# A planned two-filter FFT kernel on one core: F in one transfer, an inverse step on the full array, a last row in halves, and a new order

## The chip, the cores and the metric

The kernel runs on one core of a Trainium2 chip. The time is the device time of one execution in microseconds (us); lower is better. A core has five instruction streams that run side by side and meet only at semaphores: TensorE (PE, matrix products into PSUM), VectorE (DVE), ScalarE (ACT), GpSimd (POOL, unused here but for start-up) and SyncE (SP), which issues nearly all DMA transfers here. The transfers themselves are carried by 16 DMA engines.

## The reference

Input `x` is 2048 rows (S) by 1024 columns (D) in bf16; `gate_w` has 1024 values; `A_w_r`, `A_w_i`, `B_w_r`, `B_w_i` are real and imaginary parts of two filters of 2048 by 513. `B_x` is not used.

```
g = sigmoid((x * gate_w).sum(-1, keepdims=True))
X = rfft2(x)                      # over rows and columns
a = irfft2(X * (A_w_r + 1j*A_w_i)).bfloat16
b = irfft2(X * (B_w_r + 1j*B_w_i)).bfloat16
out = g * a + (1 - g) * b
```

One forward transform serves both filters; the two inverse transforms are mixed row by row with the gate `g`.

## The kernel before, in words

All transforms are matrix products with constant matrices (`make_consts`), in five stages. The 2048 rows are split as 128 partitions by 16 values of `n2`; the row transform is done in two factors, 128 and 16.

**S1** (`xrows`, `stage_s1`). `x` comes in eight transfers of two `n2` values (512 KB) each (`xload`). VectorE folds every pair of rows about the middle column (`fS`, `fT`: sum and difference, four rows of 256 a call). TensorE then multiplies by the constant `F` (the factor-128 transform), 8 matmuls of 256 columns per `n2`; every product needs `F` and `-F`, and `C["F"]` holds both, 1 MB, loaded in four pieces `FP` between the loads of `x`. For `n2` 14 and 15 (`FULL`) VectorE folds once more (`u0`, `u1`) and 8 matmuls of 128 columns do. The result is copied from PSUM to SBUF (`Z`), by ScalarE or VectorE. `gate_row` uses 32-column matmuls for the gate.

**D and S2** (`stage_d`, `stage_s2`), per group `kg` of 16: the column transform (8 matmuls of 256 and two of 1 column, copy `Q`), then the factor-16 row transform (4 matmuls of 512 columns, copy `X`).

**Products and I1** (`prod`, `stage_i1`), per filter `b` and pair of groups `m` (8 of each): VectorE multiplies `X` by the filter (two `mul` of 2048 elements per partition, two `sum` of 1024 that subtract or add the halves). For the pairs in `SPLIT` the two `sum` are left out and TensorE does them with twice the matmuls. `I1`, the first inverse step, is done twice per pair, for the two halves `h` of `n2`: the matmuls give 64 output rows each, for the two groups of the pair on the two halves of the array's columns (`64 * r`, "128*64" in the profile). The result is copied to a buffer `ub` (`V`, 1024 elements per partition) and "turned": a DMA from SBUF to SBUF takes the 128 partitions of `ub` to 16 partitions of the buffer that the next stage reads (one `turn` of 256 KB per `h`, 32 in all).

**S** (`inverse`), per `n2`: `Sj0`, `Sj1` and `Sk1` (16 matmuls of 128 columns) give the mixed rows, copy `T`; `Dinv` (8 matmuls of 256) is the inverse column transform, copy `o`; VectorE unfolds with four add or subtract calls (`h0`, `h1`, `y0`, `y1`) for two `n2` at a time (one at a time for 14 and 15), and SP writes the rows out. All rows with `n2` below 8 need every turn with `h` = 0, the others every turn with `h` = 1.

**The order.** `P.add` collects 518 nodes. `Plan.run` simulates the five engines; the string `TABLE` gives, for each node in order of creation, its engine (p, a, v, g, s) and its due place, by which a free engine picks among the nodes that are ready. Buffers come from pools with limits (`ub`: 10 at a time) in a ring of 32 cells. `Sched.emit` writes each engine's instructions in the resulting order with semaphore waits. Which engine copies what, and when, is thus fixed in the program; on the chip only waits decide. Nearly all instructions are recorded at the lines of helpers: L493 (matmuls), L496 (VectorE on two tensors), L518 and L519 (copies by ScalarE and VectorE), L524 (DMA issues), so the profile's groups are told apart by tile names and shapes.

Of the kernel before, what the change touches and what calls it, by code (L numbers as in the profile page):

```python
# [10 lines left out]
AP = bass.AP  # L11
# [6 lines left out]
v80 a100 s90 s145 s200 s255 s310 s365 s420 s475 s530 s585 s640 s695 a240 s750 s805 s860 s915 s978 s1105 s1168 s1295  # L18
s1358 s1421 s1484 s1548 s1611 s1674 s1737 s1801 s1864 s1927 s1990 s2054 v90 p160 a612 p1815 a1862 v505 v444 p666
v774 p578 a712 v611 v672 p840 a953 p753 a861 v888 v948 p1022 a1130 p1109 a1222 v1088 v1028 p1284 a1405 p1197 a1313  # L20
v1305 v1244 p1378 a1496 p1466 a1588 v1379 v1439 p1640 a1771 p1553 a1679 v1513 v1573 p1728 a1869 p1839 v1947 v1708
v1648 v1782 v1855 p1970 a2039 p2070 a2135 p1926 a1991 p2058 p2014 v2091 p2166 p2114 v2199 p2288 p2245 a2321 p2393
v2426 p2508 v2532 s2109 s2172 s2298 s2362 s2488 s2551 s2615 s2678 s2741 s2804 s2868 s2931 s2994 s3057 s3121 s3184
p2300 a2414 p2523 a2631 p2414 a2529 p2703 v2810 v3052 v3226 v2939 v3166 p3501 a3636 s3745 p3328 a3453 s3562 p2610
a2724 p2883 a2995 p2789 a2904 p3062 a3178 v3288 v3515 v3401 v3575 p3767 a3910 s4020 p3681 a3819 s3928 p2969 a3087
p3242 a3361 p3149 a3270 p3415 a3544 v4096 v4270 v3983 v4210 p4477 a4642 s4752 p4387 a4551 s4660 p3587 a3727 p3853
a4002 p3940 a4093 p4206 a4368 v4792 v5019 v4905 v5079 p5372 a5509 s5618 p5192 a5326 s5435 p4294 a4459 p4569 v4678
p4660 a4774 p4933 a5051 v5487 v5714 v5600 v5774 p5897 a6009 s6119 p5983 a6101 s6210 p4840 a4960 p5106 a5234 p5278
a5417 p5551 a5692 v6062 v6235 v5948 v6175 p6737 a6870 s6979 p6478 a6595 s6705 p5458 a5600 p5724 v5834 p6069 a6192
p6391 a6504 v6870 v6997 v7057 v7184 p7353 a7466 s7575 p7439 a7557 s7666 p6184 a6298 p6650 a6778 p6298 a6412 p6564  # L30
a6687 v7258 v7372 p7698 a7892 s8001 p7526 a7719 s7829 v6984 p7168 v7245 v7833 v7846 v8467 v8477 v8533 v8520 v8559
v8546 v6296 v6523 v6409 v6583 p6823 a6961 s7071 p6909 a7053 s7162 v3635 v3862 v3749 v3923 p4033 a4185 s4294 p4119
a4276 s6412 v4444 v4618 v4330 v4557 p4753 a4866 s4975 p5019 a5143 s6539 v5253 v5427 v5139 v5366 p5638 a5783 s5893
p5810 a5918 s6476 v8199 v8373 v8086 v8313 p8456 v8569 s8698 p8698 v8805 s8934 v7599 v7772 v7485 v7712 p7871 a7984
s8093 p7957 a8075 s8184 v6757 v6643 p6996 a7189 s7299 p7180 a7374 s7483 v7859 v7972 p8284 a8477 s8587 p8111 a8305
s8414 p8543 a8619 p8653 v8704 v8746 p8587 v8683 p8829 v9070 v9328 s6602 p8044 a8167 v8433 v8487 p8565 a8760 v8919
v8966 p8066 a8966 v9036 v9083 p8089 a8569 v8713 v8760 p8784 p9148 p9208 a9260 p9410 a9519 p9630 p9719 p9798 a9824
p9941 v10073 v10247 v10308 v10381 v10556 s10629 p8853 p9103 p9187 v9214 p9537 a9645 p8934 p9064 p9142 a9169 p9278
v9387 v9825 v9765 v9899 v10187 s10261 p10118 p10202 p10336 a10362 p10474 a10586 p9366 p9498 p9624 v9651 p9803 a9916
v10797 v10736 v10917 v11038 s11111 p9675 p9759 p9891 v9959 p10386 a10495 p9896 p10029 p10113 a10139 p10248 v10442  # L40
v10616 v10676 v10857 v10977 s11051 p10341 p10561 p10645 a10678 p10827 a10952 p10068 p10163 p10241 a10268 p10650
a10769 v11158 v11098 v11232 v11406 s11480 p10600 p10738 p10822 a10861 p11133 a11246 p10777 p10915 p10999 a11044
p11226 a11337 v11466 v11527 v11600 v11723 s11797 p11004 p11088 p11220 v11292 p11446 a11554 p10954 p11049 p11128
a11154 p11313 a11429 v11663 v11784 v11857 v11931 s12005 p11401 p11533 p11617 a11645 p11755 a11863 v11991 v12025
v12072 v12173 s12220 p11572 p11638 p11698 a11737 p11857 a11966 v12106 v12139 v12207 v12254 s12301"""
# [13 lines left out]
def make_consts():  # L59
# [14 lines left out]
    C["F"] = np.stack([F, -F], 2).reshape(128, 4096)  # L74
# [68 lines left out]
    KI = KI.reshape(2, 2, 128, 2, 2, 8, 8).transpose(2, 0, 1, 3, 4, 6, 5).reshape(128, 1024)  # L143
# [140 lines left out]
class Node:  # L284
    def __init__(self, name, key, engs, build, reads, writes, after, alloc, dma):
        self.name, self.key, self.engs, self.build = name, key, engs, build
        self.reads, self.writes, self.after, self.alloc, self.dma = reads, writes, after, alloc, dma
        self.pre, self.place = set(), 0


class Plan:


    def __init__(self, arena, limit):
# [4 lines left out]
        self.free0 = (0.8, 1.0, 0.8, 0.8, 0.9)  # L299

# [20 lines left out]
    def run(self, table):  # L321
# [21 lines left out]
        dma_free = 0.0  # L343
# [100 lines left out]
def bass_gated_mix__spectral_gfnet__spectral_gfnet__prompt_kernel(  # L444
# [60 lines left out]
    def pe(name, ns, build, reads, writes, alloc=(), **kw):  # L505
        return P.add(name, cost(ns), lambda e: build(), reads, writes, alloc=alloc, **kw)
# [434 lines left out]
```

## Time and profile before

| what | value |
|---|---|
| median of 3 runs | 132.09 us (132.0 to 132.16) |
| the profiled execution, its own time | 131.37 us |
| its span, from the first to the last instruction | 129.5 us |
| mean granted TensorE clock | 0.991 |
| PE, DVE, ACT busy | 117.5, 107.5, 100.2 us |
| DMA | 14064 packets, 28.62 MB, 221 GB/s on average |

A row such as "L496 DVE TENSOR_TENSOR RING<-R 128x2048" is one group of instructions: the line of the helper, the engine, the operation, the tensor written, the tensors read and the shape (partitions by elements). `R` stands for the large SBUF tensors R1 to R5 (`x`, the constant `F`, the filters, `X`, the turned data and the last stage's buffers), `RING` for the ring of small buffers, `PS` for PSUM. A busy time counts overlapping instructions once. The end of a matmul is modelled: a single one of 512 columns is recorded as 0.38 us, while its successor starts 0.216 us after it.

### The profile page before, as it was taken

The numbers are of one execution on the slowest core, as the hardware profiler recorded it, in microseconds if no ns is written. First come the engines' busy times: TensorE is split into PE (matmuls) and PEld (weight loads), VectorE is DVE, ScalarE is ACT, GpSimd is POOL, SyncE is SP. The second block draws the span as 40 slices with busy tenths as digits, with TensorE's granted clock in tenths as the row PEclk, the third lists the DMA queues.
The fourth block names the chain that finished last, engine by engine and source line by source line (L and its number), as shares of the span: only waits on it lengthen the run. The fifth ranks groups of instructions, "written<-read, shape, count | busy, mean of one in ns | idle before, by whom it ended". The sixth has DMA issues, their size and how long they took to land.

```text
span 129.5 us, 2793 instructions
## 1 busy us (share of the span) xinstructions
PE 117.5 (91%) x1149; PEld 76.6 (59%) x1149; DVE 107.5 (83%) x155; ACT 100.2 (77%) x109; POOL 0.2 (0%) x4
## 2 busy tenths in 40 slices
PE   6687999899999999999999999999969999999710
PEld 2365786566544455445483555555659999999600
DVE  1386796417999997998899999998965899999992
ACT  4348898597999997999799958667335659999950
POOL 0000000000000000000000000000000000000000
PEclk9999999999999999999999999999999999999996
DMA  4999999999999997406348998987630004435474
GB/s 116 289 379 419 407 418 372 378 378 387 382 380 372 218 193 180 132 0 161 90 128 217 289 209 190 221 200 168 172 81 5 0 0 167 162 149 197 173 297 162
DMA packets 14064, 28.62 MB, mean 221 GB/s; under 512 B 1506, under 2 KB 5858, under 8 KB 14051
## 3 DMA queue, kind: packets, MB, share of 16 engines
q1 hardware_dynamic: 14048, 28.44, 70.2%
q8 instruction: 9, 0.15, 0.5%
q14 instruction: 5, 0.03, 0.1%
q10 hardware_dynamic: 2, 0.00, 0.0%
HBM read 15.85 MB, written 4.19 MB: 155 GB/s over the span
## 4 chain that ended last, share of the span: by engine, by line
PE 60%; DVE 20%; DMA 9%; issue 3%; SPq 3%; ACT 2%; DVEq 0%
PE PS L493 60%; DVE R L496 14%; DMA R<-in_A_x_dram 7%; DVE R L519 4%; SPq L524 3%; DMA R<-RING 3%; ACT R L518 2%; DVE RING L496 1%; DVE RING L519 1%; ACT RING L518 1%; DVEq L248 0%; DVE V L519 0%
## 5 line engine op out<-in xcount | busy, mean ns | idle before, releaser
L518 ACT ACTIVATE R<-PS 128x1024 bf16<-128x1024 f32 x52 | 50.9, 1028 | 12.9 <-PE PS L493 12.7
L518 ACT ACTIVATE RING<-PS 128x1024 bf16<-128x1024 f32 (+1 forms) x48 | 46.7, 1008 | 8.8 <-PE PS L493 8.8
L496 DVE TENSOR_TENSOR RING<-R 128x2048 bf16<-128x2048 bf16 (+1 forms) x48 | 47.8, 1043 | 6.2 <-DMA R<-in_A_x_dram 6.1
L493 PE MATMUL PS<-RING,SK 128*64 128x512 bf16 (+1 forms) x368 | 51.2, 382 | 0.1
L493 PEld LDWEIGHTS PS<-RING,SK 128*64 128x64 bf16 (+1 forms) x368 | 21.5, 108 | 24.3 <-issue 6.7
L493 PE MATMUL PS<-DM,R 128*128 128x256 bf16 (+1 forms) x256 | 27.4, 245 | 0.5 <-DMA R<-RING 0.5
L493 PEld LDWEIGHTS PS<-DM,R 128*128 128x128 bf16 x256 | 18.9, 97 | 5.7 <-issue 2.1
L519 DVE CAST R<-PS 128x1024 bf16<-128x1024 f32 (+1 forms) x16 | 15.2, 961 | 8.1 <-PE PS L493 8.1
L496 DVE TENSOR_TENSOR R<-R 128x1024 bf16<-128x1024 bf16 (+1 forms) x36 | 20.6, 626 | 0.3
L496 DVE TENSOR_TENSOR RING<-RING 128x1024 bf16<-128x1024 bf16 x28 | 18.2, 684 | 0.1
L493 PE MATMUL PS<-DI,R 128*128 128x256 bf16 x128 | 16.1, 273 | 1.3 <-ACT R L518 1.3
L493 PE MATMUL PS<-R,RING 128*128 128x256 bf16 (+1 forms) x128 | 14.5, 266 | 2.6 <-DVE RING L496 2.6
L493 PEld LDWEIGHTS PS<-R,RING 128*128 128x128 bf16 x128 | 11.4, 98 | 6.0 <-DVE RING L496 4.5
L493 PEld LDWEIGHTS PS<-DI,R 128*128 128x128 bf16 x128 | 11.7, 98 | 3.0 <-ACT R L518 1.6
L493 PE MATMUL PS<-RING,R 128*128 128x128 bf16 x128 | 9.3, 219 | 0.0
L493 PEld LDWEIGHTS PS<-RING,R 128*128 128x128 bf16 x128 | 7.7, 98 | 0.6 <-DVE R L519 0.4
L493 PE MATMUL PS<-MS,R 128*128 128x1 bf16 (+1 forms) x40 | 5.2, 165 | 0.0
L519 DVE CAST RING<-PS 128x512 bf16<-128x512 f32 (+1 forms) x4 | 3.8, 958 | 1.6 <-PE PS L493 1.5
L493 PE MATMUL PS<-RING 128*128 128x512 bf16 x8 | 3.5, 615 | 1.2 <-DVE RING L588 1.2
L493 PEld LDWEIGHTS PS<-MS,R 128*128 128x128 bf16 (+1 forms) x40 | 3.4, 96 | 0.4 <-issue 0.2
L844 ACT ACTIVATE RING<-PS 128x512 bf16<-128x512 f32 x4 | 2.4, 601 | 1.1 <-DVE RING L496 1.1
L493 PE MATMUL PS<-R,G 128*32 128x512 bf16 x32 | 2.5, 384 | 0.4 <-ACT R L518 0.4
(34 smaller groups left out, 17.7 us busy)
## 6 DMA issues: line engine op xcount, KB each, us to landing
R<-RING SPq DMA_DIRECT2D x32, 256.0 KB, 4.4
R<-in_A_x_dram SPq DMA_DIRECT2D x8, 512.0 KB, 8.3
out_dram<-R SPq DMA_DIRECT2D x7, 512.0 KB, 2.6
R<-in_A_w_r_dram SPq DMA_DIRECT2D x7, 256.5 KB, 9.6
R<-in_A_w_i_dram SPq DMA_DIRECT2D x7, 256.5 KB, 9.5
R<-in_B_w_i_dram SPq DMA_DIRECT2D x7, 256.5 KB, 8.1
R<-in_B_w_r_dram SPq DMA_DIRECT2D x7, 256.5 KB, 8.2
R<-c_F SPq DMA_DIRECT2D x2, 320.0 KB, 7.6
```

Of the source, the lines that this page charges most:

```text
L493: return lambda e: e.matmul(o, l, r, start=start, stop=stop, skip_group_check=True)
L496: return lambda e: e.tensor_tensor(out=o, in0=a, in1=b, op=op)
L518: return [lambda e: e.activation(o, i, ACT.Copy)]
L519: return [lambda e: e.tensor_copy(o, i)]
L524: lambda e: [lambda q, d=d, s=s: q.dma_start(d, s) for d, s in pairs()],
L844: P.add("sig", {"act": (0.5, 0.7)}, lambda e: [lambda e: e.activation(rg(gr, 0, [[1, 512]]), psl(t, 0, [[1, 512]]), ACT.Sigmoid)], [(t,)], ...
```

## The change: what it does

1. `F` alone is loaded, 512 KB in one transfer after the first two rows of `x`; VectorE makes `-F` in two calls (`FN`, 256 and 1792 elements per partition). `S1` waits for both.
2. For `n2` 0, 1, 14 and 15 (`SINGLE`) the folds are done one row at a time (four calls of 512 elements in place of two of 1024).
3. `I1` takes one group at a time on the whole width of the array (128 output rows). `KI`'s columns are reordered so that the two halves `h` lie on alternate partitions of the result, and each result is turned in two transfers of 128 KB, each from every second partition (64) to 8 partitions: 64 in all.
4. The last pair (1, 7) (`LATE`) goes in smaller parts: four `mul` of 1024 elements, `I1` in three calls per group, copies `V` of 512.
5. The last row, `n2` = 15, is finished in halves (`finish`): `Dinv`, the copy (`oh`, 512), `h0` and `h1` (256) are done twice, `y0` and `y1` (512) write two tiles, and two transfers of 128 KB take them out, one of them in pieces of 256 elements.
6. `Sj1` and `Sk1` are one call except in the first two rows of each half; one warm-up matmul fewer is issued; the pools change (`ub` 10 to 5, `q` 4 to 2, `st` 3 to 4 and others); `TABLE` has 554 new entries. In it VectorE has 13 copies of 1024 elements (3 `Z`, 2 `Q`, 1 `X`, 3 `T`, 4 `o`) and two `V` of 512, before 14 (2 `Z`, 3 `X`, 2 `V`, 4 `T`, 3 `o`).

```diff
-SPLIT = ((0, 7), (1, 6), (1, 7))
+SPLIT = ((0, 7), (1, 6))
+LATE = ((1, 7),)
+SINGLE = (0, 14)
-FP = ((0, 2), (2, 6), (6, 11), (11, 16))
+NEG = (0, 2, 16)
...
-    C["F"] = np.stack([F, -F], 2).reshape(128, 4096)
+    C["F"] = F.reshape(128, 2048)
...
-    KI = KI.reshape(2, 2, 128, 2, 2, 8, 8).transpose(2, 0, 1, 3, 4, 6, 5).reshape(128, 1024)
+    KI = KI.reshape(2, 2, 128, 2, 2, 8, 8).transpose(2, 0, 1, 3, 6, 5, 4).reshape(128, 1024)
...
-             {"ps": ("ps", 4), "p1": ("ps", 8), "sj": ("ps", 3), "st": ("ring", 3), "u": ("ring", 1), "q": ("ring", 4),
-              "t": ("ring", 2), "tn": ("ring", 4), "pp": ("ring", 2), "g": ("ring", 1), "gz": ("ring", 1), "RA": ("ring", 1), "ub": ("ring", 10), "w": ("ring", 1), "T": ("t", 4),
+             {"ps": ("ps", 4), "p1": ("ps", 8), "sj": ("ps", 3), "st": ("ring", 4), "u": ("ring", 2), "q": ("ring", 2),
+              "t": ("ring", 2), "tn": ("ring", 2), "tl": ("ring", 4), "pp": ("ring", 4), "g": ("ring", 2), "gz": ("ring", 2), "RA": ("ring", 1), "ub": ("ring", 5), "w": ("ring", 1), "T": ("t", 4),
...
     xload(*DEPTH[0])
-    for i, (a, b) in enumerate(FP):
-        cload("sp", R2, a * 256, "F", a * 256, b * 256, [("F", j) for j in range(a, b)])
-        if i + 1 < len(DEPTH):
-            xload(*DEPTH[i + 1])
-    for a, b in DEPTH[len(FP) + 1:]:
+    cload("sp", R2, 0, "F", 0, 2048, ["F"])
+    for a, b in DEPTH[1:]:
         xload(a, b)
...
+    for a, b in zip(NEG, NEG[1:]):
+        P.add("FN", {"dve": (0.07 + (b - a) * 0.034, 0.2 + (b - a) * 0.034)}, lambda e, a=a, b=b: [lambda e: e.tensor_scalar(
+            out=ap(R2, 2048 + a * 128, [[1, (b - a) * 128]]), in0=ap(R2, a * 128, [[1, (b - a) * 128]]), scalar1=-1.0, scalar2=None, op0=ALU.mult)],
+            ["F"], [("FN", i) for i in range(a, b)])
...
+        if (b, m) in LATE:
+            p = PT[b, m] = [[Tile("tl", 2) for _ in range(2)] for _ in range(2)]
+            for kg in range(2 * m, 2 * m + 2):
+                P.key = ("PA", "PB")[b], m
+                for c, t in enumerate(p[kg % 2]):
+                    P.add("mul", vt(1024), lambda e, t=t, c=c, kg=kg: [tt(
+                        rg(t, 0, [[512, 2], [1, 512]]), ap(R4, kg * 1024, [[512, 2], [1, 512]]),
+                        ap(T, kg * NS + c * NW, [[NW - 2 * c * NW, 2], [1, 512]]), ALU.mult)],
+                        [("X", kg)] + wkeys(b, (kg,)), [(t, 0, 2)], alloc=[t])
+            return
...
+        def turns(u, kg, parts=1):
+            for h in range(2):
+                def turn(h=h):
+                    return [(AP(T, (64 * (kg % 2) + m) * pt + h * 8192, [[8 * pt, 8], [1024, 8], [1, 1024]]),
+                             AP(RING, h * pit[id(RING)] + u.at * CELL, [[2 * pit[id(RING)], 64], [1, 1024]]))]
+                dma("turn", "sp", turn, 0.131, 200, [(u, i * 2 // parts, (i + 1) * 2 // parts) for i in range(parts)], [("U", b, kg, h)], n=1.1,
+                    after=allz(h) if b else [("x", i) for i in range(16)])
...
+        for r in range(2):
+            kg = 2 * m + r
+            P.key = ("IA", "IB")[b], kg
             t, u = Tile("ps", 2), Tile("ub", 2)
-            def fns(h=h, t=t):
...
-                            f.append(mm(psl(t, o * 512, [[1, 512]], 64 * r, 64), ap(SK, z, [[1, 64]]),
-                                        rg(src, r * 1024 + v, [[1, 512]]), i == 0, i == len(terms) - 1))
-                return f
...
+            def fns(r=r, t=t):
+                return [mm(psl(t, o * 512, [[1, 512]]), matrix(r, i, o * 128, 128), data(r, i), i == 0, i == len(terms) - 1)
+                        for o in range(2) for i in range(len(terms))]
...
             ev("V", 1024, lambda t=t, u=u: (rg(u, 0, [[1, 1024]]), psl(t, 0, [[1, 1024]])), [(t,)], [(u, 0, 2)])
-            dma("turn", "sp", lambda u=u, h=h: [(AP(T, m * pt + h * 8192, [[8 * pt, 16], [1024, 8], [1, 1024]]), rg(u, 0, [[1, 1024]]))],
-                0.262, 205, [(u, 0, 2)], [("U", b, m, h)], n=1.15, after=allz(h) if b else [("x", i) for i in range(16)])
+            turns(u, kg)
...
+    def finish(v, o, h):
+        for p in range(2):
+            P.key = ("E", 15)
+            t = Tile("p1", 1)
+            pe("Dinv", [256] * 4, lambda p=p, t=t: [
+                mm(psl(t, c * 256, [[1, 256]]), rg(v, (c * 4 + 2 * p + i) * 128, [[1, 128]]), ap(DI, ((2 * p + i) * 2 + c) * 256, [[1, 256]]), i == 0, i == 1)
+                for c in range(2) for i in range(2)], [(v, 0, 2), "DI"], [(t,)], alloc=[t] + ([] if p else [o]))
+            ev("oh", 512, lambda p=p, t=t: (rg(o, p * 512, [[1, 512]]), psl(t, 0, [[1, 512]])), [(t,)], [(o, p, p + 1)])
+            P.key = ("U", 15)
+            a, b = rg2(o, p * 512, [[1, 256]]), rg2(o, p * 512 + 256, [[1, 256]])
+            P.add("h0", vt(256), lambda e, p=p, a=a, b=b: [tt(rg(h, p * 512, [[1, 256]]), a(), b(), ALU.add)], [(o, p, p + 1)], [(h, p, p + 1)], alloc=[] if p else [h])
+            P.add("h1", vt(256), lambda e, p=p, a=a, b=b: [tt(rg(h, p * 512 + 511, [[-1, 256]]), a(), b(), ALU.subtract)], [(o, p, p + 1)], [(h, p, p + 1)])
...
+            d = outv[:, 15, 256:768] if i else AP(outv.tensor, outv[:, 15, 0:256].offset, [list(outv[:, 15, 0:256].ap[0]), [768, 2], [1, 256]])
+            dma("out", "sp", lambda y=y, d=d: [(d, rg(y, 0, [[1, 512]]))], 0.131, 400, [(y, 0, 1)], [], kind="out", n=0.65)
```

More of the change, by code (lines that the diff above doesn't have):

```diff
@@ L575, in wpart @@
         dma("W%d" % b, "sp", lambda: parts, 0.2627, 335, [], [("W", b, g, c, pm)], n=1.15 * len(parts),
-            after=[("F", i) for i in range(16)] if b and c == 0 and g < 2 else [])
+            after=["F"] + [("FN", i) for i in range(16)] if b and c == 0 and g < 2 else [])
     def wkeys(b, kgs=range(16)):
@@ L754, in stage_i1 @@
         pt = pit[id(T)]
[L755 to L776 removed]
+        wide = isinstance(p, list)
@@ L820, in v512 @@
             ev("U5", 8, lambda h=h: (ap(UR[b], 512 + h * 8192, [[1024, 8]]), psl(t2, h * 8, [[1, 8]])), [(t2,)], [("U5", b, h)], only="dve",
-               after=[("U", b, m, h) for m in range(8)])
+               after=[("U", b, kg, h) for kg in range(16)])
     for kg in range(16):
@@ L874, in inverse @@
             P.key = ("E", n2)
+            if last:
+                break
             def inv(t=t2, v=v):
```

149 lines of the change are left out of this document (91 added, 58 removed), and 2 rows, old and new, of the table P.

## The prediction

> **What bounds the kernel now.** I read the page first: its busy times, slices and chain.
>
> ```profile
> PE 117.5 (91%) x1149; PEld 76.6 (59%) x1149; DVE 107.5 (83%) x155; ACT 100.2 (77%) x109; POOL 0.2 (0%) x4
> PE   6687999899999999999999999999969999999710
> DVE  1386796417999997998899999998965899999992
> PE 60%; DVE 20%; DMA 9%; issue 3%; SPq 3%; ACT 2%; DVEq 0%
> ```
>
> See: PE is full from slice 5 to 28 (16 to 90 us), but DVE is nearly as full there, so PE alone does not set that stretch. The start waits for transfers; the end (slices 34 on) is DVE's. The timelines show the four places where this change acts. VectorE at the start:
>
> ```profile
> 4.33 1.29 DVE L496 TENSOR_TENSOR RING<-R 128x1024 bf16<-128x1024 bf16 x2 [3.18 <-DMA R<-in_A_x_dram]
> 6.82 1.29 DVE L496 TENSOR_TENSOR RING<-R 128x1024 bf16<-128x1024 bf16 x2 [1.19 <-DMA R<-in_A_x_dram]
> ...
> 11.48 1.29 DVE L496 TENSOR_TENSOR RING<-R 128x1024 bf16<-128x1024 bf16 x2 [0.90 <-DMA R<-in_A_x_dram]
> 13.59 5.14 DVE L496 TENSOR_TENSOR RING<-R 128x1024 bf16<-128x1024 bf16 x8 [0.81 <-DMA R<-in_A_x_dram]
> ```
>
> See: up to 13.59 each pair of rows waits for `x`, with pieces of `F` queued between. TensorE in the middle, one I1 between two groups D:
>
> ```profile
> 56.64 0.60 PE L493 MATMUL PS<-DM,R 128*128 128x256 bf16 x4
> 57.16 1.05 PE L493 MATMUL PS<-RING,SK 128*64 128x512 bf16 x8
> 58.15 0.50 PE L493 MATMUL PS<-DM,R 128*128 128x256 bf16 x3
> ```
>
> See: four matmuls of 256 columns follow one another at 0.109 us, so I1 could start at 57.07; it starts at 57.16. Its four pairs could take 4 x 0.216 = 0.86; D starts after 0.99. Going to half-width matmuls and back costs 0.09 + 0.12 = 0.21 to 0.22 us. And VectorE's only two waits between 31.13 and 88.14:
>
> ```profile
> 49.50 1.22 DVE L519 CAST R<-PS 128x1024 bf16<-128x1024 f32 x1 [0.89 <-PE PS L493]
> ...
> 62.10 1.22 DVE L519 CAST R<-PS 128x1024 bf16<-128x1024 f32 x1 [0.94 <-PE PS L493]
> ```
>
> Last, the chain of waits at the turn to the last stage:
>
> ```profile
> 89.97 1.22 DVE RING L519
> 91.19 0.03 DVE V L519
> 91.22 3.49 DMA R<-RING
> 94.71 0.05 issue
> 94.76 1.10 PE PS L493 x15
> ```
>
> See: the last products end at 88.14, the copy `V` at 91.19, its turn lands at 94.71, and only then the rows of S run on.
>
> **The change part by part.** The sum goes against the profiled execution, 131.37 us (span 129.5 plus 1.87 around it); the median of the runs is 0.72 above it.
>
> *Start.* In the trace the transfers land thus: x0 4.31, F 4.79, x1 6.80, F 7.96, x2 9.27, F 10.09, x3 11.38, F 12.21, x4 13.49, then one `x` every 1.28 to x7 at 17.34. New: x0 4.31, F (512 KB, as one `x`) 5.6, x1 6.9, then every 1.28: x4 10.7, x7 14.6. The first S1 comes later: F at 5.6 and `FN` for two rows, so 5.9 in place of 5.68. The second pair: 6.9 + 1.29 of folds = 8.2, as before (8.17). From there `x` (1.28) and folds (1.29) come faster than TensorE uses them (16 x 0.109 = 1.75 a pair), so six pairs end at 8.2 + 10.5 = 18.7, gfold 0.35 and the short pair 0.9 make 20.0. Before, S1 ends at 23.04 with two gate blocks and the products behind one in it (about 1.5): 21.5 for the same work. Gain 1.5. If the early rate (1.16 us for 256 KB of F) holds for the new F too, it lands at 6.6 and the gain is 0.8; without any wait 2.0. `FN` has no row: nearest are tensor-by-tensor calls, 1.09 us for 1792 elements by 0.69 per 1024 and 1.22 per 2048; from below 0.27, the one-source MEMSET. It lies between 5.9 and 6.9, where VectorE waits for x1: 0, at most 0.3. `SINGLE` adds two calls of about 0.1 twice, under the same waits. The missing warm-up matmul falls in an idle second (4.7 to 5.68): 0; if the clock were granted late, the first pair would run at the warm-ups' 0.427 per 512 columns, 1.75 more, 1.2 of it uncovered.
>
> *Middle.* There are 16 such visits to half width: TensorE is relieved of 16 x 0.22 = 3.5 us; the matmuls themselves are as long (a pair of halves 0.216, a full one 0.216). But VectorE works from 31.13 to 88.14 with 1.83 us of waits, and its work there does not shrink: three copies as before (2 `Q`, 1 `X` for 3 `X`), `LATE` 4 x 0.61 for 2 x 1.15 (+0.1). So at most 1.8 reaches the last product. Five visits (1.1 us) lie ahead of either wait, which would close both; another order may open others: I take half, 0.9 (0 to 1.8).
>
> *Turns and the passage to S.* SP issues 32 transfers more; one takes 0.53, 0.64 from start to start without a pause. In the last stretch, 16 turns from 73.41 to 93.60, 32 halves at 0.64 make 20.5 us in 20.2: SP just keeps up (0 to 0.6 late). A half turn is 0.64 us of transfer by bytes: ten whole turns land 1.19 apart from 79.62 to 90.29, and the sole one has 1.28. After the last `sum`, before 6.6 us pass until S runs on. New: I1 on one group 0.87, the other 0.87, its copy by ScalarE 1.03, three semaphore hops 0.1 to 0.2: 3.0; its first half turn then lands 2.4 after issue (3.0 for a whole one in the trace, less 0.64): 5.4. Gain 1.2; the other half queues behind three more issues (1.9), 7.3, where before the second half landed at 96.6, 8.5 after. Bounds 0 and 2.
>
> *S and the end.* From 100.69 to 127.0 VectorE never stops. It has seven copies as before; row 15 in halves gives 4 x 0.27 + 2 x 0.34 for 4 x 0.34: 0.3 more. The copies `oh` come 0.4 earlier and the last transfer is half as long (0.3 less). Together 0 (0.5 either way).
>
> Sum: 1.5 + 0.9 + 1.2 + 0 = 3.6; 131.37 - 3.6 = 127.8 for a profiled run, 128.5 for the median.
>
> **The rivals.**
>
> *A half turn costs as much as a whole one.* Then 32 of them at 1.2 take 38.4 us where 20.2 are there: 18 us later, 146.5. The gain is used up from 0.64 + 3.6/32 = 0.75 us on. Five buffers `ub` instead of ten would carry the delay back to TensorE. For it: the target has 8 partitions instead of 16, no row shows such a shape. Against it: the bytes halve, and the same 16 engines bring an `x` of 512 KB in 1.28, so a turn of 256 KB in 1.19 to 1.28 is not at their limit. Chance 0.17.
> [...]
> [...]
>
> *VectorE keeps the stretch.* The middle's waits only move and the passage gains nothing since SP's queue is late: only the start is left, 132.09 - 1.5 = 130.6. For it: 1.83 us of waits in 57. Against: both waits are for TensorE. Chance 0.22.
>
> *All of it pays.* 2.0 + 1.8 + 2.0 = 5.8: 126.3. Chance 0.06. *Nothing moves:* what the start gains is lost in a new order: 132.1, chance 0.03.
>
> **How the numbers follow.** My forecast has 0.52 and a range of its own of 127.0 to 130.3 (132.1 less 5.1 and less 1.8: start 2.0, middle 1.8, passage 1.3 against 0.8, 0.4, 0.6). The range for 8 in 10 leaves out the first rival and the edge of the third: 126.4 to 132.0. Two runs of this kernel differ by some 0.1%; 0.2% (0.26 us) is what can be told. Faster: 0.52 + 0.22 + 0.06, less 0.02 for the edge of the second, 0.78; same 0.03; slower 0.17 + 0.02 = 0.19.
>
> **What would show it.** F lands near 5.6 and x7 near 14.6; D's first matmul comes near 23 (before 24.81, with more gate work ahead of it). The middle has no half-width I1 and VectorE's span of products is 55 to 56 us. Turns land 0.6 to 0.7 apart when queued; S runs on 5 to 6 us after the last product. Wrong it would be if queued turns land over 0.75 apart, with TensorE waiting for copies `V` whose buffers are not free, or if VectorE waits for TensorE at new places in the middle. [...]

## The result and the profile after

The changed kernel takes 156.44 us (median of 4 runs, 155.74 to 156.96); the kernel before took 132.12 us beside it (132.0 to 132.3). The ratio is 1.1835, with a 95% interval of 1.1774 to 1.1897: 18% slower, where 128.5 us was forecast. Times of one kernel on one chip scatter by up to 0.7% either way (23 runs of the kernel before: 130.99 to 132.8 us), the changed kernel's relatives by more; where a ratio stands beside medians that don't match it, it leaves out disturbed runs, those more than 1.5% above the kernel's fastest.

The page of the changed kernel: the busy times, four of its slice rows (one slice is 3.86 us), the packets and the chain by engine.

```profile
PE 123.5 (80%) x990; PEld 79.5 (52%) x996; DVE 109.4 (71%) x164; ACT 99.9 (65%) x113; POOL 0.2 (0%) x4
...
PE   6599999999999765499767499519639999999930
...
PEclk9999999999999999879999969996995699999998
DMA  5999999999635555135855555555555000453337
GB/s 145 399 406 414 355 380 377 389 377 377 230 96 104 105 106 107 36 94 120 157 140 116 124 111 112 120 113 115 130 163 163 2 4 0 179 232 140 140 144 265
DMA packets 13902, 28.08 MB, mean 182 GB/s; under 512 B 1473, under 2 KB 6081, under 8 KB 13890
...
DMA 30%; PE 28%; DVE 20%; ACT 11%; issue 4%; SPq 4%; DVEq 0%; ACTq 0%
```

See: the engines' work is about the same as before (PE 123.5 for 117.5, part of it at a lower clock), but the span grew by 24.7 us and DMA now leads the chain (30%, before 9%). From slice 11 on (42 us) only half of the DMA engines' time is used, at 94 to 120 GB/s in most slices: these are the turns. Before, the stretch from 70 to 90 us ran at 214 GB/s. In the windows of the kernel before and then of the changed one (columns: stretch, its length, busy time of PE, PEld, DVE, ACT, POOL, granted clock, DMA share, GB/s):

```profile
70.00:90.00 20.00, 20.00 (x186) 10.20 (x184) 19.50 (x32) 15.40 (x17) 0.00 (x0) 1.00 0.95 214
```

```profile
70.00:90.00 20.00, 14.22 (x62) 5.81 (x62) 13.47 (x17) 11.69 (x15) 0.00 (x0) 0.95 0.60 132
90.00:115.00 25.00, 16.24 (x79) 6.92 (x79) 14.30 (x25) 10.87 (x15) 0.00 (x0) 0.91 0.53 122
115.00:125.00 10.00, 9.72 (x109) 8.97 (x110) 4.71 (x12) 3.13 (x4) 0.00 (x0) 0.66 0.24 74
```

See: TensorE and VectorE, almost without a pause before, stand for 30 to 40% of the time; and when the last stage starts (115 to 125 us), TensorE's granted clock is 0.66. What they wait for is in the list of waits of the changed kernel (us in total, times, the longest); the first and third lines have no counterpart before:

```profile
ACT RING L528 <- DMA R<-RING: 21.3, 12, 3.4
...
PE PS L501 <- ACT RING L528: 14.6, 9, 3.5
...
DVE RING L504 <- DMA R<-RING: 12.0, 4, 5.3
```

See: the copies `V` wait for a buffer `ub` whose turns have not landed, TensorE waits for those copies, and VectorE's products wait for cells of the same ring that turns have not freed. The chain names the same transfers; four of its pieces (start, length, what):

```profile
51.60 10.35 DMA R<-RING
...
82.06 10.58 DMA R<-RING
...
95.03 8.98 DMA R<-RING
...
105.77 7.45 DMA R<-RING
```

See: a half turn takes 7 to 10 us from its issue, because seven to nine others that were issued before it have not landed yet; with none ahead the first one took 3.3. The records of the trace give the price of one: in a queue the last packets of successive half turns come some 1.2 us apart (68.6, 69.7, 70.8, 71.9, 73.2), the landings 0.9 to 1.4, with eight engines at work and a median of 165 ns for a 2 KB packet. All 64 of them, 8.39 MB, take from 43.4 to 119.7 us; before, the same bytes took from 41.8 to 96.1.

| kernel | last product ends | last packet of a turn | span |
|---|---|---|---|
| before | 88.1 | 96.1 | 129.5 |
| changed | 105.7 | 119.7 | 154.2 |
| changed, partitions 4 apart, ten warm-ups (below) | 86.0 | 95.9 | 129.7 |

### The profile page after: what moved, and what is told of

The parts are those of the page before. It is cut to its first block, busy times and chain, and to the rows that moved or that the text cites. A ratio compares the mean times of both kernels' runs of the same rounds, so it can differ in the third digit from the quotient of the medians.

```text
span 154.2 us, 2529 instructions
## 1 busy us (share of the span) xinstructions
PE 123.5 (80%) x990; PEld 79.5 (52%) x996; DVE 109.4 (71%) x164; ACT 99.9 (65%) x113; POOL 0.2 (0%) x4
## 4 chain that ended last, share of the span: by engine, by line
DMA 30%; PE 28%; DVE 20%; ACT 11%; issue 4%; SPq 4%; DVEq 0%; ACTq 0%
PE PS L501 28%; DMA R<-RING 28%; DVE R L504 10%; DVE RING L504 7%; ACT RING L528 7%; ACT R L528 4%; SPq L534 4%; DMA R<-in_A_x_dram 2%; DVE R L529 2%; ACT RING L893 1%; DVEq L266 0%; DVE DM L504 0%; DVE R L602 0%; ACTq L252 0%; DVEq L252 0%
## 5 line engine op out<-in xcount | busy, mean ns | idle before, releaser
L501 PE MATMUL PS<-RING,SK 128*128 128x512 bf16 x210 | 54.8, 406 | 17.5 <-ACT RING L528 13.4
L504 DVE TENSOR_TENSOR RING<-R 128x2048 bf16<-128x2048 bf16 (+2 forms) x54 | 48.7, 946 | 25.2 <-DMA R<-RING 12.0
L528 ACT ACTIVATE R<-PS 128x1024 bf16<-128x1024 f32 (+1 forms) x54 | 52.3, 1017 | 17.5 <-PE PS L501 17.5
L501 PEld LDWEIGHTS PS<-RING,SK 128*128 128x128 bf16 x216 | 21.0, 103 | 45.7 <-ACT RING L528 12.9
L504 DVE TENSOR_TENSOR R<-R 128x1024 bf16<-128x1024 bf16 (+2 forms) x38 | 20.8, 603 | 0.3
L529 DVE CAST R<-PS 128x1024 bf16<-128x1024 f32 (+1 forms) x15 | 14.1, 947 | 6.0 <-PE PS L501 4.0
L501 PEld LDWEIGHTS PS<-R,RING 128*128 128x128 bf16 x128 | 12.3, 104 | 5.5 <-DVE R L602 2.7
L501 PE MATMUL PS<-RING,R 128*128 128x128 bf16 x128 | 10.8, 239 | 0.1
L529 DVE CAST RING<-PS 128x1024 bf16<-128x1024 f32 (+1 forms) x5 | 5.6, 1117 | 7.3 <-DMA R<-RING 4.3
L501 PEld LDWEIGHTS PS<-RING,R 128*128 128x128 bf16 x128 | 9.1, 108 | 0.5 <-DVE R L529 0.4
```

The costliest lines, as they stand in the source:

```text
L501: return lambda e: e.matmul(o, l, r, start=start, stop=stop, skip_group_check=True)
L504: return lambda e: e.tensor_tensor(out=o, in0=a, in1=b, op=op)
L528: return [lambda e: e.activation(o, i, ACT.Copy)]
L529: return [lambda e: e.tensor_copy(o, i)]
```

## The experiments

**Where the eight partitions lie.** A half turn has half the bytes of a whole one and costs as much. Was it the number of DMA engines (8 for 16), the places that it writes, or a fixed price? The two kernels here change only the numbering of the partitions of the turned data (with the rows of `RM`, the gate and the 512th column that go with it); sizes, outer counts, engines and order stay. The changed kernel writes eight partitions 8 apart, the two others eight 4 apart and eight side by side. The labels and the expectations call these layouts four, eight and two ports; a "port" there is a set of places taken to share a rate, the author's assumption, and no record shows one.

```diff
-AP(T, (64 * (kg % 2) + m) * pt + h * 8192, [[8 * pt, 8], [1024, 8], [1, 1024]])
+AP(T, (kg % 4 + 32 * (kg // 4)) * pt + h * 8192, [[4 * pt, 8], [1024, 8], [1, 1024]])   # 4 apart
+AP(T, (8 * kg) * pt + h * 8192, [[pt, 8], [1024, 8], [1, 1024]])                         # side by side
```

> The changed kernel, with another numbering of the partitions that the turns write: half turn kg goes to partitions kg mod 4 + 32 (kg div 4) + 4e, e = 0 to 7, in place of 64 (kg mod 2) + kg div 2 + 8e. Everything else stays, the shapes, the sizes and the outer counts of 64 and 8 too. Theory 1, the places of the target: the eight old partitions collide in pairs on the way into SBUF and the new ones do not; half turns land 0.62 to 0.70 us apart when queued (2 KB packets near 84 ns, as alone in the changed kernel), the waits for RING disappear, and the kernel takes 127 to 131 us, my forecast. [...] Theory 2, the number of DMA engines: it is still 8, so half turns stay 1.2 us apart and the time at 156 us. Theory 3, a fixed price of such a transfer whatever its layout: as theory 2.

> The changed kernel with the eight partitions of a half turn next to one another: 8 kg + e. [...] Theories 2 and 3 (number of engines, fixed price): 1.2 us and 156 us as before this edit.

Measured: 4 apart 130.86 to 135.65 us, median 133.02 of 12 (ratio 0.9947, 0.9906 to 0.9988), most of them above the 127 to 131 expected; side by side 220.63, in a single run. Their windows, first 4 apart, then side by side:

```profile
70.00:80.00 10.00, 9.00 (x41) 3.62 (x40) 8.84 (x11) 7.69 (x10) 0.00 (x0) 1.00 0.52 193
```

```profile
60.00:70.00 10.00, 5.73 (x26) 2.42 (x24) 0.00 (x0) 3.88 (x4) 0.00 (x0) 0.66 0.54 58
```

See: the DMA share is the same 0.52 to 0.54, eight engines of 16, in both and in the changed kernel; the rate is 193 and 58 GB/s, against 105 to 120. A 2 KB packet takes 84, 314 and 165 ns. So neither the number of engines nor a fixed price is the cause: the target's places are, by a factor of two a step. What it is in the places that sets the rate is not shown. (The changed kernel goes from partitions below 64 to those from 64 on, or back, every few half turns, and between 45 and 64 us the next one lands somewhat sooner where it does: 1.1 us after the last, 1.4 in the same half. From 89 to 106 us this is not so: there a step to the other half lands 1.3 after the last, and one in the same half 0.9 to 1.3. Each of the last twelve goes to the other half, or to the other four of every eight partitions, than the one before it, and they land 0.8 apart.)

**The half turns alone.** Does the price act by itself, without the new inverse step and its five buffers?

```diff
-dma("turn", ... [(AP(T, m * pt + h * 8192, [[8 * pt, 16], ...]), rg(u, 0, [[1, 1024]]))], ...)
+dma("turn", ... [(AP(T, (64 * r + m) * pt + h * 8192, [[8 * pt, 8], ...]), rg(u, 0, [[1, 1024]], 64 * r, 64)) for r in range(2)], ...)
```

> The kernel before with one edit: each whole turn of 128 partitions into 16 is cut into two transfers, 64 partitions into 8 each, to the same places; the first inverse step, its column tiles, the ten buffers and the order stay. If the half turns alone are the cause: two halves take 2 x 1.2 = 2.4 us where one whole turn took 1.19; 32 pairs take 77 us from about 36 us on, so the last lands near 113 in place of 95 us, and the kernel takes 148 to 156 us. If the cause is rather the new first inverse step, its order or its five buffers: 132 to 136 us (twice the issues on SP only).

Measured: 137.98 to 144.21, median 140.65 (ratio 1.047, 1.0412 to 1.0529). Slower by 6 to 12 us, so half turns do cost by themselves; but the size was missed, and the reason is in the order of the targets: here the two halves in a row go to different halves of the partitions, below 64 and from 64 on, and from 80 us on the queue runs at 170 to 190 GB/s:

```profile
80.00:100.00 20.00, 18.35 (x191) 10.05 (x188) 17.07 (x32) 11.99 (x15) 0.00 (x0) 1.00 0.53 182
```

Two more runs vary that alone: one numbers the partitions so that eight half turns in a row stay in one half of the partitions and in the same four of every eight, one puts the eight 4 apart as above.

```diff
-(64 * r + m) * pt, [[8 * pt, 8], ...
+((2 * m + r) % 8 + 64 * (m // 4)) * pt, [[8 * pt, 8], ...          # the same places
+((2 * m + r) % 4 + 32 * ((2 * m + r) // 4)) * pt, [[4 * pt, 8], ... # 4 apart
```

> The kernel before with its turns cut into halves, four ports each as in the first such run, but numbered so (kg mod 8 + 64 (kg div 8) + 8e) that both halves of a turn, and the next turns too, go to the same four ports; in the first such run they alternated between two sets of four, and queued half turns came to 190 GB/s in places. If it is the ports: now 105 to 110 GB/s throughout as in the changed kernel, a half turn 1.1 to 1.2 us, 64 of them 70 to 77 us from 39 us on, and the kernel takes 148 to 158 us. If the numbering of turns in a row does not matter: 138 to 144 as in the first such run.

> The kernel before with its turns cut into halves as in the earlier run, and the new numbering of the target partitions. Ports alone: a pair of halves falls from about 2.0 us to 1.34 (2 x 8 packets of 84 ns), against 1.19 for the whole turn; in the last stretch 16 turns at 1.34 take 21.4 us where 20.2 to 21.2 are there, so 132 to 134 us, and SyncE is busy 1.3 of each 1.28 us. If something else in half turns costs time (a fixed price, the issues): 136 us or more as with four ports (138).

Measured: the same places 159.5 (158.87, 160.12), 4 apart 136.61 (135.74 to 137.8). The windows of the first:

```profile
50.00:70.00 20.00, 16.35 (x112) 7.17 (x112) 14.68 (x17) 13.20 (x14) 0.00 (x0) 0.91 0.49 105
...
90.00:115.00 25.00, 17.86 (x142) 8.55 (x138) 13.16 (x26) 10.44 (x13) 0.00 (x0) 0.86 0.54 113
```

See: 105 to 113 GB/s here (120 from 70 to 90 us), as in the changed kernel, and a loss of 27 us, with the old inverse step, ten buffers and the old order. So a loss of the size of the changed kernel's 24 us needs neither the new inverse step nor five buffers, only half turns that queue for the same places; how often they do depends on the order, which lies between this run's and the alternating one in the changed kernel. The expectation for 4 apart (132 to 134) was missed: packets of 174 ns still occur among those of 84 (the slowest tenth, 70 to 80 us), and the rate is only 179 from 80 to 90. This kernel reads 64 partitions in a row where the changed one reads every second; whether the source side is the reason was not tried.

**What is left without the turns.** If the turns are all that went wrong, the kernel with the partitions 4 apart and half the bytes should come out at the forecast.

```diff
-[[4 * pt, 8], [1024, 8], [1, 1024]]  <-  [[2 * pit[id(RING)], 64], [1, 1024]]
+[[4 * pt, 8], [1024, 8], [1, 512]]   <-  [[2 * pit[id(RING)], 64], [1, 512]]
```

> The changed kernel on eight ports, each half turn with only the first 512 of its 1024 columns (64 KB; the other columns of the turned rows are left as they were, so a half of what the last stage reads is not the first stage's result). Everything else stays: 64 issues, eight engines, eight ports. If the rate of the turns (195 GB/s on eight engines) is what still separates the eight-port kernel (131 to 134) from my forecast, the last turn lands 2.5 to 3 us after its issue and the kernel takes 129 to 130; what SyncE's 64 issues cost stays in it (last issue still near 93 to 94). If other parts of the change are worth nothing or less: 131 to 133 as before.

Measured: 129.1 (two runs, 128.48 and 129.73; ratio 0.9781, 0.973 to 0.9832). Its half turns, 64 KB each, carry half of the bytes that the forecast priced at 0.64 us, and the last three land 0.3 to 0.4 us apart; those of the 4-apart kernel, 0.67, are near the forecast's price. Its last turns and those of the 4-apart kernel, from the two chains (first half the bytes, then all):

```profile
89.37 3.80 DMA R<-RING
93.20 0.20 DVE R L532
93.41 0.05 issue
93.45 7.33 PE PS L504 x97
```

```profile
94.00 5.46 DMA R<-RING
99.51 6.83 PE PS L504 x88
```

See: with half the bytes VectorE works from 31 us to the end of its products without a wait for a turn (84.9 us, 3.2 before the old 88.1), and the last stage runs on at 93.45. With all bytes it runs on at 99.51 in this run: turns at 190 GB/s, 0.67 us each, still hold it.

The last turns of these two chains show something else. The half turns issued from 41 to 89 us land 2.1 to 2.4 us after their issue in the kernel with half the bytes; the one issued at 89.37 takes 3.80. Seven of its eight engines post their end by 91.48, the eighth at 93.18. The only packet there that is not a turn's is one of 16 KB, at 90.51, from another queue than the one of SyncE's transfers, and it takes 1.29 us. The start alone (below), the kernel before and five of the other runs show the same with the packet that comes between 89 and 97 us: of a turn then in flight, one engine posts its end 0.9 to 1.9 us after the others (1.4 of the 5.46 us in the second chain above). The records don't say which engine carries the packet; that it holds up this one engine fits, and is not shown.

**SyncE's queue, and the buffers.** SyncE issues half turns 0.655 us apart in the 4-apart kernel, in stretches of several us without a pause. The first edit makes one transfer of both halves (the inverse matrix's rows reordered), the second takes half its bytes too, the third allows eight `ub`.

```diff
-for h in range(2): ... [[4 * pt, 8], [1024, 8], [1, 1024]] <- [[2 * pit[id(RING)], 64], [1, 1024]]
+[[4 * pt, 8], [1024, 16], [1, 1024]] <- [[pit[id(RING)], 128], [1, 1024]]
...
-"ub": ("ring", 5)
+"ub": ("ring", 8)
```

> The changed kernel on eight ports, with the two half turns of a group made one transfer of 256 KB, 128 partitions into 8 (the inverse matrix gives its rows in the order that this needs). SyncE issues 32 turns in place of 64. In the eight-port run SyncE issued half turns without a pause, 0.655 us apart, from 81.4 to 87.3 us and again to 94.0, three to four microseconds after their data was copied, and the last one landed 5.46 us after its issue. If SyncE's queue is what holds the passage: the last turn lands 3 to 4 us earlier than 99.5 and the kernel takes 128.5 to 130 us. If the eight engines are (8 packets of 84 ns each for a half, 0.67 us, 1.34 for the whole, the same rate as SyncE's 0.655 a half): under 1 us better than the eight-port kernel, 130.5 to 132.5.

> The eight-port kernel with one transfer for both halves of a group, and only the first 512 columns of each row (as in the run beside it, half of what the last stage reads is not written). 32 issues and half the bytes: neither SyncE's queue nor the rate of the turns is left. If these two are all that stood between the eight-port kernel and my forecast: 128 to 129.5. If the time stays above 131, the new first inverse step, its order or the start hold it, and my terms for the middle and the passage were wrong for another reason than the turns.

> The changed kernel on eight ports, with up to 8 buffers ub in place of 5. In the eight-port run copies V waited for turns to free a buffer: 3.4 us in all on ScalarE, 2.3 + 1.8 on VectorE, and TensorE stood 1 us at 71.8 behind it. If the buffers are on the path: those waits go and the time falls by 1 to 2 us, with less scatter. If turns are late by their own rate: the waits go, the turns queue instead, and the time stays within 0.5 us.

Measured: 136.71 (134.64 to 138.73), 131.57 (130.56, 132.58) and 133.31 (132.46 to 133.75). One transfer in place of two gains nothing, with all bytes or with half, and half the bytes are worth 4 to 5 us in both forms. That the single transfer loses 2.5 to 4 us against the two was not expected; both halves land together, and the planner's order changes in some ten places on each of TensorE, VectorE and ScalarE, and these causes were not told apart. So these runs don't settle what SyncE's queue costs. The kernel with half the bytes and 64 issues tells a little: SyncE issues there without a pause from 67.2 to 90.68 us, though the last copy `V` ends at 88.22, so its queue ends some 1.8 us late (an estimate: two issues after the copy would end near 88.9), and the kernel takes 129.1 all the same. More buffers gain nothing either (its order differs in a few places at the end, so no more than that is read from it).

**The parts that have nothing to do with turns.** The new start alone on the kernel before, and the new end alone:

```diff
+    cload("sp", R2, 0, "F", 0, 2048, ["F"])     # and FN, SINGLE, seven warm-ups: start alone
...
+        if last:
+            return finish(v, o, h)               # end alone
```

> The kernel before with only the new start: F in one transfer, negated on VectorE, the folds of the first and last pair by single rows, seven warm-up matmuls; the engine times of the rest stay as in the old table. My prediction's term: the first D comes 1.5 us earlier and, if VectorE has no new waits, 1.5 us of it arrive at the end (130.6). Rival: the stretch behind it is held by something else and the order after it was laid out for the old start, so less than 0.5 us arrive (131.6 to 132.3).

> The kernel before with only the new end: row 15 in halves, with two transfers out of 128 KB. My prediction put the last stage and the end at 0 with 0.5 either way: 131.4 to 132.5 us. Rival: the shorter last transfer and the earlier copies pay more than the 0.3 us of extra work on VectorE, 131.0 to 131.4.

Measured: start alone 131.13 against 131.95 (ratio 0.9945, 0.9911 to 0.9978), end alone 132.03 against 131.91 (1.0016, 0.9997 to 1.0035). The end is worth nothing, as forecast. The start pays 0.8 of 1.5 us. In its trace the first D comes at 24.08 (before 24.81; the changed kernel, with gate work moved behind it, 23.25) and VectorE is 0.73 earlier at 89 us, but its chain ends in this:

```profile
90.49 4.32 DMA R<-RING
94.80 0.05 issue
94.85 1.10 PE PS L493 x15
```

See: the turn is issued 0.73 us earlier than the 91.22 of before and takes 4.32 for 3.49, so the last stage runs on no earlier. This is no queue of turns: the turn before the last three landed 2.97 us after its issue, as one without a queue does. It is the late engine named above: a 16 KB packet comes at 90.49 and takes 1.72 us, the turn issued at 89.42 has 15 of its 16 posts by 92.55 and the last at 94.07, and this one has 15 by 93.65 and the last at 94.80. Half the bytes on the kernel before and on this one were to test whether it is the rate of the turns.

```diff
-[[8 * pt, 16], [1024, 8], [1, 1024]] <- rg(u, 0, [[1, 1024]])
+[[8 * pt, 16], [1024, 8], [1, 512]]  <- rg(u, 0, [[1, 512]])
```

> The kernel before, each turn with only the first 512 of its columns (half of what the last stage reads is not written). The last turn but one landed 3.49 us after its issue, 3.0 without a queue: 0.5 us at the passage, nothing ahead of it, so 131.2 to 131.8 if the turns' rate held it, 131.9 to 132.1 if not.

> The kernel before with the new start alone, and each whole turn with only the first 512 of its 1024 columns (half of what the last stage reads is not written). If the rate of the turns held back part of the start's gain (VectorE 0.73 us earlier at 89 us, last turns at 94.80 against 94.71): turns land 3.0 after issue, the last stage starts near 93.6, and the kernel takes 129.6 to 130.3. If not: as the start alone, 130.9 to 131.2.

Measured: 131.36 and 131.57 us against 131.99 (ratios 0.9951, 0.993 to 0.9971, and 0.9953, 0.9917 to 0.9988). For the kernel before that is the 0.6 us expected: its whole turns, 1.19 us apart in the queue, hold the passage by half a microsecond. With the new start the expectation (129.6 to 130.3) failed in eight runs of ten. The passage did get shorter (from the last copy `V`'s start at 90.70 to the first `Dinv` at 97.23 it is 6.5 us, in the start alone 89.23 to 97.05, 7.8; the late engine struck a turn here that nothing waited for, issued at 89.16), but the profiled run had lost the start's gain ahead of it: VectorE's first copy of the middle came at 30.60, in the start alone at 29.14. TensorE's timeline shows why; the start alone, then the same start with half the bytes:

```profile
6.13 1.92 PE L493 MATMUL PS<-R,RING 128*128 128x256 bf16 x16 [1.76 <-DVE R L592]
8.38 1.92 PE L493 MATMUL PS<-R,RING 128*128 128x256 bf16 x16 [0.32 <-DVE RING L496]
```

```profile
6.06 5.44 PE L493 MATMUL PS<-R,RING 128*128 128x256 bf16 x32 [1.68 <-DVE R L592]
```

See: 16 matmuls in 1.92 us (0.109 each and the last one's tail) in the one, 32 in 5.44 in the other: 1.8 us more than 32 x 0.109 and that tail. The turns have not begun there. The second pair of rows ends at 11.50, in the start alone at 10.30: 1.2 us, what the prediction had named for a clock granted late.

**The start's clock.** The prediction named this and priced it at nothing: the missing warm-up leaves TensorE idle for 1.76 us ahead of S1. Ten warm-ups in place of seven shorten that pause:

```diff
-for _ in range(7)]
+for _ in range(10)]
```

> The kernel before with the new start alone, and ten warm-up matmuls in place of seven: at 0.43 us each they end near 5.6 us, 0.4 us ahead of the first matmul of S1 (6.1), where seven left a pause of 1.76 us and the eight of before one of 1.0. If the pause is what lets the first matmuls run slowly: 16 matmuls in 1.92 us in the profile, and the runs gather at the lower end of the start alone's 130.4 to 132.4: median 130.4 to 130.8. If not: the same spread, median near 131.1.

> The eight-port kernel once more, unchanged, for a profile of one of its faster runs: 130.9 to 135.7 us. In the run profiled before, the last turn landed at 99.5 us after a queue on SyncE (half turns issued 0.655 apart) and on the engines. If the rate of the turns is what varies, a faster run shows the last turn landing at 96 to 97 us with the products on VectorE as early; if something else varies, the landing is the same and the loss lies behind it.

> The changed kernel on eight ports, with ten warm-up matmuls in place of seven. If late clocks at the start make its spread (130.8 to 136.8, median 133): median 131 to 132 and no run over 134. If the spread comes from the turns in the middle: median 132.5 to 133.5 as before this edit.

Measured: start with ten warm-ups 130.84 (130.38 to 131.89; ratio 0.9932, 0.9905 to 0.9959); 4 apart again, with seven, 132.94 (130.81 to 136.75); 4 apart with ten 131.25 (129.7 to 132.91; ratio 0.9919, 0.9888 to 0.995). The 4-apart kernel's spread above 133 is gone. The second profile of it with seven warm-ups has a granted clock of 0.50 from 8 to 10 us; with ten, S1 begins as in the second view:

```profile
8.00:10.00 2.00, 2.00 (x11) 1.35 (x10) 1.59 (x3) 1.02 (x2) 0.00 (x0) 0.50 1.03 420
```

```profile
6.35 1.92 PE L504 MATMUL PS<-R,RING 128*128 128x256 bf16 x16 [1.51 <-DVE R L605]
```

See: at full rate, 0.109 us a matmul, from the first. Of the eleven profiles with seven warm-ups two begin so, the changed kernel's not among them (24 matmuls in 4.34 us: 0.213 each up to 9.35 us, 0.109 from 9.48 on); of the seven with eight warm-ups four do, with pauses of 0.9 to 1.2 us in all; both with ten do. The trace's records of the granted clock sort all twenty profiles. In the eight quick ones full clock begins at 3.9 to 6.0 us and holds far beyond the start. In nine late ones it begins only at 9.0 to 10.7 us, the changed kernel's at 9.38 (a stretch without a record counts as 1.00 in the clock row, so the row doesn't show it). In the other three late ones it begins at 3.9 to 4.0, is taken back to 0.50 at 7.3 to 7.5 for 3.41 us, and then full again. But for the last of each run, every recorded stretch is a multiple of 3.41 us long (122.88 in the kernel before; from 3.41 to 54.61 in the changed one). Which of the three happens is not set by the pause alone: with full clock from about 4 us, pauses of 1.23 and 1.51 us kept it and pauses of 1.94 to 2.29 lost it; with full clock from 4.80 a pause of 1.76 kept it. What else sets it is not shown.

**Alternating whole turns.** If the places that it writes hold a whole turn at some 200 GB/s (214 from 70 to 90 us before), two in a row to different places should run at once. The second half of each group goes to the other four of every eight partitions:

```diff
-AP(T, m * pt + h * 8192, [[8 * pt, 16], ...
+AP(T, (m ^ 4 * h) * pt + h * 8192, [[8 * pt, 16], ...
```

> The kernel before with the new start, and whole turns as before, but the second half of a group goes to the partitions with bit 2 flipped, so that two turns in a row write partitions that the first left free (R's second 1024 columns, the gate's row and the 512th column follow). In the run with the new start alone VectorE was 0.7 us earlier at 89 us, but the last turns landed at 94.80 where they landed at 94.71 before: they queue 1.2 us apart. If the rate of the turns holds the start's gain back: queued turns land 0.65 to 0.9 us apart, the last stage starts 1 us earlier, and the kernel takes 129.7 to 130.5. If 195 GB/s is a limit of something else than the target's ports (the source, the engines): no change against the start alone, 130.6 to 131.2. [...]

> The kernel before with only the alternating places of the two halves. The last turn but one landed 3.49 us after its issue, and one without a queue takes 3.0: at most 0.5 us at the passage, so 131.4 to 131.9 if the ports hold the queue, no change if not. Queued turns land 0.65 to 0.9 us apart by the first theory, 1.19 by the second.

Measured: with the new start 133.22 (131.25 to 133.69; ratio 1.0003, 0.997 to 1.0036); on the kernel before 138.19 (137.25 to 138.68), but there the larger constant `MS` changed the planner's order (24 differences on TensorE, some 45 on VectorE), so it tells nothing of places. In the first, whose order is that of the start alone, turns land 0.6 to 1.3 us apart (80.03, 81.03, 81.66, 82.73, 83.98, 85.21), but they are issued 0.9 to 2.0 apart, so their spacing is that of the issues and not of a queue. They did wait less: issued from 79.5 us on they land 3.2 to 3.9 us later, in the start alone the same turns 3.9 to 4.6 (without a queue 3.0), and a 2 KB packet takes 112 ns for 153 between 80 and 90 us. That agrees with the first theory in kind. Whether two whole turns to different places run at once at full rate stays open, since the issues here come too seldom for a queue, and why the kernel is no quicker does too; its profile is one with a late clock (32 matmuls in 5.00 us, first D at 25.41 for 24.08).

## Why the prediction was wrong

The rival that it gave 0.17, a half turn at the price of a whole one, is what happened.

*The failed step* is "A half turn is 0.64 us of transfer by bytes". It measured about 1.2 (0.9 to 1.4) in a queue with the partitions 8 apart, and 0.67 with them 4 apart. The argument against the rival, that an `x` of 512 KB lands in 1.28 us on the same engines, compared a target of 128 partitions with one of eight. The row that it needed was in the trace: a whole turn, 256 KB to 16 partitions, at 1.19 us, half the rate of `x`. A limit in the places that are written can leave the time as it was when partitions and bytes are both halved, and in the changed kernel's layout it did. Eight of the 16 engines carry a half turn in all three layouts (a DMA share of 0.52 to 0.54), so their number is not what cost the time.

*The rival's own sum*, 146.5, was too low by 10. It priced the last 32 half turns alone. The delay is carried by all 64: at 1.2 us each they are 77 us, and from the first packet to the last they took 76.3 (with two pauses, and the quicker ones at the end), where the old turns took 54.3. That TensorE would be held through `ub` was named; it then loses clock as well (0.66 from 115 to 125 us). But five buffers are no condition: with ten, in the old order, the same places give 159.5.

*Start*, 1.5 us: the landings came near what was written (F 5.79 for 5.6, x1 7.05 for 6.9, x7 14.96 for 14.6), the first D at 23.25. Alone it pays 0.8, with ten warm-ups 1.0 (130.84 against 131.87). Two of its steps were off: "The missing warm-up matmul falls in an idle second: 0", which costs up to 1.8 us at the first matmuls in some runs (the prediction had this price, for a clock granted late, and gave it no chance); and in the profiled run the 0.73 us that VectorE kept was lost at the passage, to the late end of one engine and not to a queue. Most of what is missing at the first D (0.73 alone where 1.5 was forecast) goes at the second and third pair of rows: the second starts at 8.38 for 8.2, and the third waits 0.41 us for its folds, which were to come faster than TensorE uses them; `x2` lands at 8.28, but VectorE makes a copy of 1.22 us first.

*Middle* (0.9) and *passage* (1.2): at the forecast's own price for a half turn, 0.67 with the partitions 4 apart, the forecast is not reached: the better median is 131.25 us, with ten warm-ups. With half the bytes the time comes near it, 129.1 for 128.5 in two runs, but not by its terms. By that profile the last product ends 3.2 us earlier (start and middle together were to bring 2.4; which of the two brought more can't be told from it), and from there to the end it takes 41.8 us where it took 41.4 (passage, S and end were to save 1.2). So the passage gave nothing. S runs on 8.5 us after the last product where 5.4 was forecast: the last copy `V` ends 3.3 after it (3.0 forecast), and then the half turn that S waits for is issued 1.1 later, in a queue that "just keeps up" but had fallen behind, and takes 3.8 instead of 2.4. With all bytes and the partitions 4 apart the passage costs still more (last product 86.0, end 43.7 us later), and TensorE's granted clock falls to 0.5 there (92.6 to 96.0 us), which it does not with half the bytes.

*S and the end*, 0: right for the end on the kernel before (1.0016); the other changes to S were not run alone.

*VectorE keeps the stretch*, the rival at 130.6: near what the start and the 4-apart kernel measure, but for another reason. What stops the 4-apart kernel short of the forecast goes away for the most part when the bytes of the turns are halved, so it is the turns and not VectorE's own work; the late clock at the start adds to it (131.25 with ten warm-ups, 133.02 with seven).

Two versions beat the kernel before, each by under 1%: the new start with ten warm-ups (130.84, ratio 0.9932) and the whole change with the partitions 4 apart and ten warm-ups (131.25, ratio 0.9919); their intervals overlap, and the first varies less.

## What to carry to other kernels

Price a transfer between partitions by what it writes to, not by its bytes (128 KB took 0.67, 1.2 or about 2.3 us here): when a row's rate is half of the best in the same trace (here 256 KB in 1.19 us against 512 KB in 1.28), find what limits it before scaling it down, since halving the bytes and the partitions together may leave the time as it is. Where a change replaces few transfers by many, sum them over the whole time in which they run, against the bytes per second that the slice rows show, and not only over the stretch at the end. And a pause ahead of TensorE's first real work is not free because nothing else is due in it: here up to 1.8 us followed it, in some runs.

## What the runs showed of the hardware

- The same 128 KB on the same eight engines take 0.67, about 1.2 or about 2.3 us in a queue, with nothing changed but which eight partitions they go to: 4 apart, 8 apart or side by side (190, 105 to 120 and 58 GB/s; the 2.3 is an estimate, 128 KB at 58 GB/s).
- The order of the places counts too: half turns to partitions 8 apart reached 170 to 190 GB/s where they alternated between partitions below 64 and from 64 on (140.65 us), and 105 to 120 where eight in a row kept to the same places (159.5). In the changed kernel the last twelve half turns, which change places at every step, land 0.8 us apart, most of the others in a queue 0.9 to 1.4.
- In the changed kernel, where TensorE waited for turns, its granted clock was lower: 0.95 from 70 to 90 us (1.00 before) and 0.91 from 90 to 115. It was 0.66 over the first 10 us of the last stage, so time is lost behind the turns too.
- The first matmuls after the warm-up ran at 0.109 us or at nearly twice that, in the same kernel, from run to run; three more warm-ups took the late runs away (4-apart kernel: highest 136.75 before, 132.91 after). The records of the granted clock go with it: full from 3.9 to 6.0 us on in the quick profiles, only from 9.0 to 10.7 in most late ones, or taken back for 3.41 us.
- A turn that is in flight when a 16 KB packet of another queue comes (0.9 to 1.7 us long) can land 0.9 to 1.9 us late, because one of its engines ends late: 3.80 us for 2.2 with half the bytes, 4.32 for 3.0 in the start alone. That it is the engine that carried the packet is not shown.
